# Storing five more output tiles by two DMAs each, in an attention kernel followed by a gated feed-forward

## The chip, the cores and the metric

The kernel runs on one core of a Trainium2 chip. A core has five engines that each work through an instruction queue of their own: TensorE (PE) multiplies matrices into PSUM, VectorE (DVE) and ScalarE (ACT) copy and combine, GpSimd (POOL) copies and issues loads, and SyncE (SP) only issues DMAs and waits. Engines meet through semaphores: an instruction waits until a count is reached, and adds to a count when it is done. The metric is the device time of one execution in microseconds; lower is better. The median of three runs before the change is 219.91 us (219.3 to 221.04).

## The reference, cut to what matters

Batch 8, 8 heads, 512 positions, head width 64, 32 state rows per batch and head; the feed-forward is 512 to 1536 to 512.

```python
a  = softmax(x @ state.T / 8);   xread = a  @ state     # (8, 8, 512, 64)
a2 = softmax(state @ x.T / 8);   sread = a2 @ x         # (8, 8,  32, 64)
t  = concatenate([xread, sread], axis=2)                # 544 rows per batch
t  = t.transpose(0, 2, 1, 3).reshape(8 * 544, 512)
out = (maximum(t @ w_gate, 0) * (t @ w_val)) @ w_out    # (4352, 512) float32
```

## The kernel before, in words

The value product of the attention is folded into the two first weights: for each batch `u_mm` multiplies the state rows by `w_gate` and `w_val` (the tile `U`), and `gv_mm` (line 325) multiplies `U` by the transposed attention weights `ans`. So one group of four matmuls gives the gate and the value of 128 of the 1536 hidden features for the 512 positions of a batch. `relu` (line 354, ACT) and `mult` (line 358, DVE) make the hidden tile `h_sb` from them, and `out_mms` (line 367, PE) multiplies `h_sb` by `w_out`, 128 positions at a time, twelve matmuls to an output tile. The 256 state rows of all batches go through `gvs` (line 347) at the end.

The order of the work is written out by hand. The first batches are a long list of steps (lines 462 to 490). From there a loop (line 561) goes over batch and feature group (`g = 12 * b + jf`); the table at lines 532 to 559 says behind which group the attention of the next batches, the loads and the transposes are put. The output matmuls lag 18 groups behind, in pieces of four (`out_piece`). Three pieces make one tile, and `fin_x` copies it out of PSUM on ACT (line 375) into one of eight `o_sb` buffers and stores it from SP (line 379). There are 32 such tiles, numbered here `4 * b + tsub` from 0 to 31; `fin_x` does 0 to 30. Tiles 23 to 27 are stored by two DMAs of 64 partitions each, the others by one of 128 partitions. Behind the loop come the two tiles of state rows (`fin_s`, lines 381 to 387, which stores from SP and ACT by turns), tile 30, and tile 31 in four column pieces (`out_last`, lines 389 to 400): 256 and 128 columns copied by ACT, 64 and 64 by DVE, stored by SP, ACT, SP, ACT.

SP's queue also holds the DMA transposes: `e_sn<-eT` (line 202), `ans<-a_sn` (line 226), `xT<-xb` (line 154) and `hs_sb<-sn` (line 279). SP's queue around tiles 18 to 22 is: transpose `e_sn` of batch 7, store 18, store 19, transpose `ans` of batch 7, store 20, transpose `hs_sb<-sn` of batches 6 and 7, stores 21, 22, and then the halves of 23.

The DMAs that SP and ACT issue are counted on eight semaphores, dealt out in turn over both queues in the order of the program; each such DMA first waits until the one eight before it has landed. The kernel has 75 of them, so its last one, ACT's store of the last 64 columns of tile 31, counts on the third semaphore (75 = 9 * 8 + 3). At the end of the program (shown under line 605) SP alone waits for all transfers to have landed: a first wait for two of the semaphores of POOL's loads, then eight waits, one for each of the eight semaphores from first to eighth (each paired with another count), then a drain. After that follow a barrier of the five engines, a clearing of the semaphores by POOL, and a second barrier.

Of the kernel before, what the change touches and what calls it, by code (L numbers as in the profile page):

```python
# [16 lines left out]
def kernel(  # L17
# [11 lines left out]
    B, H, S, D = x.shape  # L29
# [340 lines left out]
    def out_rows(b, tsub):  # L370
        return out[b * SP: b * SP + S].rearrange("(p q) m -> q p m", q=NC)[tsub]

    def fin_x(b, tsub, eng="act"):
        o_sb = opool.tile([128, d_model], FP32, name="o_sb", tag="o_sb")
        copy[eng](out=o_sb, in_=held["o", b, tsub])  # L375
        n = 2 if 4 * B - 9 <= 4 * b + tsub < 4 * B - 4 else 1
        for i in range(n):
            rows = slice(128 // n * i, 128 // n * (i + 1))
            nc.sync.dma_start(out=out_rows(b, tsub)[rows], in_=o_sb[rows])
# [26 lines left out]
    def out_piece(b, i):  # L406
        out_part(b, i)
        if i % 3 == 2:
            fin_x(b, i // 3)
# [41 lines left out]
    def x_load_behind(b, gb, gj):  # L451
# [7 lines left out]
             "c": c_unit, "co": c_out, "u": u_unit, "uo": u_out, "gv": gv, "gg": lambda b, jf: g_part(b, jf, 0, (0, 1)), "gw": lambda b, jf: g_part(b, jf, 1, (0, 1)),  # L459
             "ga": lambda b, jf: g_part(b, jf, 0, (0,)), "gb": lambda b, jf: g_part(b, jf, 0, (1,)), "wa": lambda b, jf: g_part(b, jf, 1, (0,)), "wb": lambda b, jf: g_part(b, jf, 1, (1,)), "re": relu, "mu": mult, "o": out_part,  # L460
             "of": fin_x, "xd": x_trans_dma, "ad": att_aT_dma, "xp": x_pad, "sr": lambda b: sr_mm((b,)), "sn": lambda b: sr_norm((b,))}
    program = """
    dx.1.0.2 dx.1.1.2 stc.0.1.dve stc.0.0.dve dw.0.0.128 dw.1.0.128 dw.0.128.128 dw.1.128.128 dw.0.256.256
# [97 lines left out]
    for g in range(first, NF * (B + 1)):  # L561
        b, jf = divmod(g, NF)
# [47 lines left out]
```

## Time and profile before

| what | value |
|---|---|
| median of 3 runs, lowest, highest | 219.91, 219.3, 221.04 us |
| time of the profiled execution | 219.11 us |
| its span, first to last instruction | 217.3 us |
| granted TensorE clock, mean | 0.998 |
| busy DVE | 134.8 us, 62% |
| busy ACT | 117.8 us, 54% |
| busy POOL | 42.5 us, 20% |
| HBM read, written | 18.35 MB, 8.91 MB |

The span is read from one execution, on the slowest (here the only) core. Between the span and the execution's own time lie 1.8 us that the profile's rows do not cover. "SPq" and "ACTq" are the queues of SP and ACT: their rows are issues of DMAs and waits, and are not counted as busy. A row such as "x10: 466/566/589, 173.3 to 194.6" says that there are ten such instructions, with shortest, median and longest duration in ns, and when the first and the last of them began in us. "DMA to landing" is the time from an issue to the last byte's arrival.

### The profile page before, as it was taken

How to read it: one execution, taken by the hardware profiler on the slowest of the kernel's cores; microseconds unless marked ns; L12 is line 12 of the kernel's file. 1: busy time of each engine (PE TensorE's matmuls, PEld its weight loads, DVE VectorE, ACT ScalarE, POOL GpSimd, SP SyncE). 2: the span in 40 equal slices, each digit the busy share in tenths (PEclk: the TensorE clock that was granted, in tenths of full speed). 3: DMA queues.
4: the chain of work that ended last, by engine and by line, in shares of the span. 5: the costliest groups of instructions: out<-in, count | busy, mean ns of one | idle time of the engine just before them, and what ended most of it. 6: DMA issues, size and time to landing. Idle time of an engine off the chain costs nothing.

```text
span 217.3 us, 4841 instructions
## 1 busy us (share of the span) xinstructions
PE 209.4 (96%) x1926; PEld 104.4 (48%) x1952; DVE 134.8 (62%) x233; ACT 117.8 (54%) x225; POOL 42.5 (20%) x63
## 2 busy tenths in 40 slices
PE   8799999999999999999999999999999999999994
PEld 4554454444444444444444444444544445666544
DVE  5799967956887778557966796388745444222100
ACT  4798887737546556455555656454646443333221
POOL 7964059005500431020107000000000000000000
PEclk9999999999999999999999999999999999999999
DMA  7999999488963996919391553131311122222132
GB/s 168 183 195 197 198 230 181 63 148 183 153 170 83 140 163 132 164 52 193 100 148 60 112 132 97 49 99 50 84 28 51 48 48 50 59 58 80 51 97 97
DMA packets 47511, 24.96 MB, mean 115 GB/s; under 512 B 27936, under 2 KB 43168, under 8 KB 47488
## 3 DMA queue, kind: packets, MB, share of 16 engines
q0 software_dynamic: 16896, 9.05, 30.8%
q1 hardware_dynamic: 29696, 14.85, 29.5%
q10 hardware_dynamic: 896, 0.75, 1.4%
q8 instruction: 15, 0.25, 0.5%
q14 instruction: 8, 0.07, 0.1%
HBM read 18.35 MB, written 8.91 MB: 125 GB/s over the span
## 4 chain that ended last, share of the span: by engine, by line
PE 93%; DMA 2%; issue 2%; ACT 1%; DVE 0%; POOL 0%; POOLq 0%
PE o_ps L367 39%; PE gv_ps L325 38%; PE gv_ps L347 5%; PE up L298 4%; DMA xb<-in_x_dram 2%; PE upc L298 2%; PE o_ps L396 1%; PE sr_ps L265 1%; PE sT_ps L189 1%; PE xT_ps L162 1%; PE sc_ps L179 1%; ACT xT L165 0%; PE aT_ps L234 0%; DVE xT L165 0%; ACT e_sn L206 0%
## 5 line engine op out<-in xcount | busy, mean ns | idle before, releaser
L367 PE MATMUL o_ps<-wo_sb,h_sb 128*128 128x512 bf16 x354 | 90.6, 379 | 2.4 <-issue 2.2
L325 PE MATMUL gv_ps<-ans,U 128*128 128x512 bf16 x377 | 92.5, 379 | 0.3
L358 DVE TENSOR_TENSOR h_sb<-gv_ps,g_sb 128x512 bf16<-128x512 f32 x96 | 65.0, 688 | 42.9 <-ACT g_sb L354 41.4
L354 ACT ACTIVATE g_sb<-gv_ps 128x512 bf16<-128x512 f32 (+1 forms) x108 | 61.8, 578 | 51.4 <-PE gv_ps L325 39.2
L325 PEld LDWEIGHTS <-U 128*128 128x128 bf16 x384 | 37.1, 98 | 44.6 <-issue 0.8
L367 PEld LDWEIGHTS <-h_sb 128*128 128x128 bf16 x372 | 35.2, 98 | 42.0 <-issue 4.0
L310 DVE CAST U<-up 128x512 bf16<-128x512 f32 x44 | 27.7, 683 | 5.7 <-PE up L298 5.7
L375 ACT COPY o_sb<-o_ps 128x512 f32<-128x512 f32 x31 | 18.4, 594 | 19.7 <-PE o_ps L367 16.7
L310 ACT CAST U<-up 128x512 bf16<-128x512 f32 x28 | 14.7, 596 | 8.8 <-PE up L298 8.8
L254 POOL COPY xa<-xb 128x1024 bf16<-128x1024 bf16 x16 | 16.0, 1044 | 10.4 <-PE sr_ps L265 5.9
L358 DVE TENSOR_TENSOR hs_sb<-gv_ps,g_sb 128x256 bf16<-128x256 f32 x12 | 5.1, 424 | 15.3 <-PE gv_ps L347 10.4
L212 DVE TENSOR_REDUCE cs<-e_sn 128x16 f32<-128x512 bf16 x16 | 10.8, 675 | 1.2 <-ACT e_sn L206 1.2
L218 DVE TENSOR_TENSOR a_sn<-e_sn,rc 128x512 bf16<-128x512 bf16 x16 | 10.9, 686 | 0.4
L298 PEld LDWEIGHTS <-stT 64*32 64x32 bf16 x560 | 6.8, 91 | 6.4 <-issue 5.3
L320 ACT CAST U<-upc 128x512 bf16<-128x512 f32 (+1 forms) x19 | 8.7, 523 | 1.7 <-PE upc L298 1.7
L453 POOL COPY mark<-g_sb 128x1 bf16<-128x1 bf16 x4 | 0.8, 190 | 41.4 <-ACT g_sb L354 41.4
L197 ACT ACTIVATE eT<-sT_ps 128x512 bf16<-128x512 f32 x10 | 5.4, 594 | 5.2 <-PE sT_ps L189 5.2
L441 POOL DMA_DIRECT2D xb<-in_x_dram x8 | 6.8, 850 | 2.9 <-issue 1.4
L347 PE MATMUL gv_ps<-br,wg_sb 128*128 128x256 bf16 x48 | 7.2, 273 | 0.1
L347 PE MATMUL gv_ps<-br,wv_sb 128*128 128x256 bf16 x48 | 7.2, 273 | 0.0
L399 DVE COPY o_sb<-o_ps 128x64 f32<-128x64 f32 x2 | 0.4, 224 | 10.6 <-PE o_ps L396 10.5
L298 PE MATMUL up<-wg_sb,stT 64*32 64x512 bf16 (+1 forms) x168 | 6.9, 348 | 0.0
(59 smaller groups left out, 122.7 us busy)
## 6 DMA issues: line engine op xcount, KB each, us to landing
out_dram<-o_sb SPq DMA_DIRECT2D x26, 256.0 KB, 2.4
xb<-in_x_dram POOLq DMA_DIRECT2D x6, 512.0 KB, 7.4
wo_sb<-in_moe_w_out_dram POOLq DMA_DIRECT2D x2, 768.0 KB, 10.7
out_dram<-o_sb SPq DMA_DIRECT2D x11, 128.0 KB, 2.3
wg_sb<-in_moe_w_gate_dram POOLq DMA_DIRECT2D x5, 256.0 KB, 9.1
wv_sb<-in_moe_w_val_dram POOLq DMA_DIRECT2D x5, 256.0 KB, 9.7
xb<-in_x_dram POOLq DMA_DIRECT2D x3, 256.0 KB, 5.1
st_f<-in_state_dram POOLq DMA_DIRECT2D x1, 384.0 KB, 11.5
```

The source lines that it names most:

```text
L212: nc.vector.reduce_sum(out=cs, in_=e_v, axis=AX.X)
L218: {"dve": nc.vector, "pool": nc.gpsimd}[eng].tensor_tensor(out=a_sn[b][:, jp].rearrange("p c (j n) -> p c j n", n=Ns), in0=e_v, in1=held[" ...
L254: nc.gpsimd.tensor_copy(out=v[:, hs], in_=xb[b][:, hs])
L298: nc.tensor.matmul(dst[kc][i0:i0 + 32], stT[r:r + 64, parity, b, h], wsb[r:r + 64, j, lo:lo + n], start=True, stop=True)
L310: copy[eng](out=U[b][:, w, kc, lo:lo + 512], in_=held["u", b, w, lo][kc])
L320: copy[eng](out=U[b][:, :, kc, lo:lo + n], in_=held["c", b, lo][kc])
L325: nc.tensor.matmul(ps[w], U[b][:, w, kc, f0:f0 + 128], ANS[b][:, kc].rearrange("p c t -> p (c t)"), start=(kc == 0), stop=(kc == NK - 1))
L347: nc.tensor.matmul(ps[w][:, 0:nt], wsb[:, j, f0:f0 + 128], br[:, j].rearrange("p b n -> p (b n)"), start=(j == 0), stop=(j == NJ - 1))
L354: nc.scalar.activation(out=g_sb[:, 0:n], in_=ps[0][:, 0:n], func=AF.Relu)
L358: nc.vector.tensor_tensor(out=dst, in0=ps[1][:, 0:n], in1=held["g", b, jf][:, 0:n], op=ALU.mult)
L367: nc.tensor.matmul(held["o", b, tsub], src[:, jf, tsub * 128:(tsub + 1) * 128], wo_sb[:, jf], start=(jf == 0), stop=(jf == NF - 1))
L375: copy[eng](out=o_sb, in_=held["o", b, tsub])
```

## The change

The range of tiles that are stored by two DMAs grows from tiles 23 to 27 to tiles 18 to 27. So five more tiles (18 to 22) are stored in two halves of 64 partitions, both issued by SP, one behind the other. The copies, the buffers and the bytes stay what they were.

```diff
     def fin_x(b, tsub, eng="act"):
         o_sb = opool.tile([128, d_model], FP32, name="o_sb", tag="o_sb")
         copy[eng](out=o_sb, in_=held["o", b, tsub])
-        n = 2 if 4 * B - 9 <= 4 * b + tsub < 4 * B - 4 else 1
+        n = 2 if 4 * B - 14 <= 4 * b + tsub < 4 * B - 4 else 1
         for i in range(n):
             rows = slice(128 // n * i, 128 // n * (i + 1))
             nc.sync.dma_start(out=out_rows(b, tsub)[rows], in_=o_sb[rows])
```

The order of instructions on PE, DVE, ACT and POOL does not change; SP has five DMAs more. SP and ACT together issue 80 DMAs (10 * 8), so the last one counts on the eighth semaphore, and every DMA behind tile 18 counts on another semaphore than before. The eight waits at the end keep their order.

## The prediction

> **What bounds the kernel now.** I read the page first: the share of each engine and the chain that ended last.
>
> ```profile
> span 217.3 us, 4841 instructions
> ...
> PE 209.4 (96%) x1926; PEld 104.4 (48%) x1952; DVE 134.8 (62%) x233; ACT 117.8 (54%) x225; POOL 42.5 (20%) x63
> ...
> PE 93%; DMA 2%; issue 2%; ACT 1%; DVE 0%; POOL 0%; POOLq 0%
> ```
>
> PE is busy 96% of the span and is 93% of the chain. Stores are not in it, so a change to stores can matter in two places only: where it makes PE wait, or behind the last matmul. So I read the stretches at the end next, each with its busy time by engine, clock, share of DMA and GB/s.
>
> ```profile
> core 0: us, PE busy (x) PEld busy (x) DVE busy (x) ACT busy (x) POOL busy (x), PEclk, DMA share, GB/s
> 210.00:214.40 4.40, 4.26 (x55) 3.23 (x54) 0.28 (x2) 1.22 (x3) 0.00 (x0) 1.00 0.42 130
> 214.40:216.10 1.70, 0.00 (x0) 0.00 (x0) 0.17 (x1) 0.00 (x0) 0.00 (x0) 1.00 0.46 125
> 216.10:216.42 0.32, 0.00 (x0) 0.00 (x0) 0.00 (x0) 0.00 (x0) 0.00 (x0) 1.00 0.00 0
> 216.42:217.32 0.90, 0.00 (x0) 0.00 (x0) 0.00 (x0) 0.00 (x0) 0.00 (x0) 0.52 0.00 0
> ```
>
> PE stops before 214.40, the last stores move until 216.10, and from there 1.2 us pass in which no engine computes and no byte moves. What fills them stands in the rows of line 605, the end of the program. First 214.50 to 216.10, then 216.11 to 216.42, then 216.15 to 216.45, then 216.48 to the end.
>
> ```profile
> L605 SPq EVENT_SEMAPHORE  x3: 28/28/28, 214.6 to 215.8; - x3
> ```
>
> ```profile
> L605 SPq EVENT_SEMAPHORE  x6: 28/28/28, 216.1 to 216.4; - x6
> ```
>
> ```profile
> L605 SPq EVENT_SEMAPHORE  x5: 28/28/28, 216.2 to 216.4; - x5
> ```
>
> ```profile
> L605 POOLq EVENT_SEMAPHORE  x4: 17/17/17, 216.6 to 217.2; - x4
> L605 SPq DRAIN  x3: 7/7/7, 216.5 to 216.8; - x3
> L605 POOLq EVENT_SEMAPHORE_RANGE_CLEAR  x1: 139/139/139, 216.9 to 216.9; - x1
> ```
>
> These nine waits of SP are the first one on POOL's loads and the eight on the store semaphores. Three of the nine are through by 215.8 (POOL's loads, first, second). The fourth is the third semaphore, on which the last store counts; it begins at 216.1. That this is where the last store lands follows from its issue and its landing:
>
> ```profile
> L400 SPq DMA_DIRECT2D out_dram<-o_sb x2: 332/341/350, 213.4 to 214.2; - x2
> L400 ACTq DMA_DIRECT2D out_dram<-o_sb x2: 357/357/357, 213.9 to 214.6; - x2
> ...
> DMA to landing us min/median/max: 1.5/1.6/1.9
> ```
>
> ACT issues it at 214.6, and with the shortest landing, 1.5 us, it is there at 216.1. Behind it five more waits begin one after the other from 216.2 to 216.4, all for counts that were reached long before, with DMA share 0.00. From the landing to the end everything is serial on SP and then on the barrier.
>
> **The change part by part.** *The last store's semaphore.* It goes from the third to the eighth. The waits for the first seven are then done while the last store is still under way: the stores issued at 213.4, 213.9 and 214.2 land within 1.9 us, by 216.1 at the latest. At the landing only the eighth wait is left, and five waits leave the path. Their price comes from their starts: six waits begin from 216.1 to 216.4, five steps in 0.3 us, 0.06 us each. So 5 * 0.06 = 0.30 us. From below, the duration of a row is 28 ns, which would make 5 * 0.028 = 0.14 us; from above, the whole stretch of 0.32 us without DMA. I take 0.30, since the starts are the serial progress itself and nothing else is in that stretch.
>
> A rule says why the row's duration is too small a price. The Trainium skill, page "Perfetto Trace Analysis", section "Per-engine timelines", says that for an instruction of the sequencer alone the profiler shows only the execution, while fetch, decode and the update of the count lie outside it. By the rows' duration the sum would be 219.77, by the starts 219.61; the starts at 0.06 beside durations of 28 ns agree with the rule.
>
> *Five more issues on SP.* Rows of the stores by one DMA (143 to 170 us) and of those already halved (172 to 196 us):
>
> ```profile
> L379 SPq DMA_DIRECT2D out_dram<-o_sb x5: 332/332/517, 144.8 to 167.6; - x5
> ...
> DMA to landing us min/median/max: 2.1/2.2/2.5
> ```
>
> ```profile
> L379 SPq DMA_DIRECT2D out_dram<-o_sb x10: 466/566/589, 173.3 to 194.6; - x10
> ...
> DMA to landing us min/median/max: 2.2/2.4/3.8
> ```
>
> A pair costs SP 0.466 + 0.589 and a gap of some 0.05 (an estimate: the step between waits above is 0.06 with 28 ns in them), 1.11 us against 0.33: each split tile holds SP 0.78 us longer, five 3.9 us. Behind tiles 21 and 22 only stores are queued. Behind 18 to 20 stand two transposes, and ahead of 18 one more:
>
> ```profile
> L202 SPq DMA_TRANSPOSE e_sn<-eT x1: 1237/1237/1237, 143.5 to 143.5; - x1
> ...
> DMA to landing us min/median/max: 3.1/3.1/3.1
> ```
>
> ```profile
> L212 DVE TENSOR_REDUCE cs<-e_sn x2: 673/674/674, 148.0 to 150.2; 128x16 f32<-128x512 bf16 x2
> ```
>
> ```profile
> L226 SPq EVENT_SEMAPHORE  x1: 1145/1145/1145, 150.8 to 150.8; - x1
> L226 SPq DMA_TRANSPOSE ans<-a_sn x1: 1254/1254/1254, 152.0 to 152.0; - x1
> ...
> DMA to landing us min/median/max: 3.1/3.1/3.1
> ```
>
> ```profile
> L325 PEld LDWEIGHTS <-U x48: 97/98/98, 161.3 to 181.6; 128*128 128x128 bf16 x48
> ```
>
> ```profile
> L279 SPq DMA_TRANSPOSE hs_sb<-sn x1: 1186/1186/1186, 156.7 to 156.7; - x1
> ...
> DMA to landing us min/median/max: 2.3/2.3/2.3
> ```
>
> ```profile
> L283 ACT COPY br<-hs_sb x2: 487/517/547, 166.4 to 166.6; 128x128 bf16<-128x128 bf16 x2
> ```
>
> The `ans` transpose is issued at 152.0, after SP has sat 1145 ns in a wait. So the 0.78 us of tile 19's second half go into that wait first and the transpose does not move. Were it late all the same: it lands at 152.0 + 3.1 = 155.1, and batch 7, whose 48 weight loads begin at 161.3, needs it 6.2 us later. The `hs_sb` transpose is late by 0.78 us, lands at 156.7 + 2.3 + 0.8 = 159.8, and ACT needs it at 166.4: 6.6 us are left. Without this cover each of the two would cost PE up to 0.78 us. The `e_sn` transpose is issued ahead of tile 18, lands at 146.6 and is read at 148.0: 1.4 us of cover, the thinnest here. Cost of all three: nothing.
>
> *Buffers and semaphores.* The second half of a tile is issued about 0.5 us later and lands in at most 3.8 us, so an `o_sb` buffer comes free up to 2.1 us later than now (0.52 + 3.8 against 2.2). ACT's copies show what this meets:
>
> ```profile
> L375 ACT COPY o_sb<-o_ps x10: 585/585/692, 161.7 to 211.7; 128x512 f32<-128x512 f32 x10
> ```
>
> ```profile
> ACT o_sb L375 <- PE o_ps L367: 7.0, 10, 0.9
> ...
> ACT o_sb L384 <- PE o_ps L367: 2.0, 1, 2.0
> ACT o_sb L384 <- DMA out_dram<-o_sb: 2.0, 1, 2.0
> ACT o_sb L375 <- DMA out_dram<-o_sb: 2.0, 1, 2.0
> ```
>
> Ten copies and the two of the state rows lie 4.5 us apart (50 us over 11 gaps); a buffer is used again eight copies later, 36 us. The two waits put down to a DMA are as long as the one for PE beside them, and I read them as waits for PE's twelve matmuls. Each DMA also waits for the one eight before it: with halves that is four tiles, 18 us, against a landing of 3.8. Both cost nothing; without the cover it would be up to 2.1 us per tile on ACT.
>
> *Sum.* On the profiled execution: 219.11 - 0.30 = 218.81 us, its span 217.3 - 0.3 = 217.0. That execution is 0.8 us under the median of the three runs, so for the median I take 219.91 - 0.30 = 219.61, rounded 219.6.
>
> **The rivals.** *Nothing is gained (219.9).* Waits for counts already reached might cost SP nothing once it starts on them earlier, or the barrier might hang on an engine other than SP. For it: 0.3 us is a third of the spread of the three runs. Against it: the five starts from 216.2 to 216.4, and the barrier's first POOL row at 216.6, behind SP's drain at 216.5.
>
> *The change doesn't do what it says.* If the last store counted on the sixth or seventh semaphore, one or two waits of 0.06 us would be left: 219.7. The count of the DMAs speaks against it.
>
> *Slower: the `e_sn` transpose lands late (221.9).* The second half of tile 18 enters the DMA engines while this transpose is still landing (143.5 to 146.6). If its landing grows by over 1.4 us, DVE stands at 148.0 with its multiplies queued behind, and PE follows. The longest landing of a transpose in this profile is 6.1 us, against 2.4:
>
> ```profile
> DMA to landing us min/median/max: 2.3/2.4/6.1
> ```
>
> That would be 3.7 late, 2.3 past the cover: 219.61 + 2.3 = 221.9. Against it: the bytes in flight are the same 256 KB as now, only in two issues.
>
> *Slower: SP's issues come onto the path (223.5).* The 3.9 us of more issue on SP would be lost in full if each issue held up what PE needs next: 219.61 + 3.9 = 223.5. It decides from where a transpose is late by more than its cover, 6.2 us for `ans` and 6.6 for `hs_sb`; the 1.6 us that tiles 18 and 19 add ahead of the one and the 2.3 of tiles 18 to 20 ahead of the other do not reach it even without SP's idle time.
>
> The Trainium skill, page "DMA: Bandwidth & Descriptors", section "Rules for kernel authors", is on the side of this rival: two transfers to disjoint halves of the partitions serialize, so one transfer of 128 is to be used. The issue rows agree that two halves are dearer.
>
> **How the numbers follow.** The forecast has a chance of 0.75, nothing gained 0.14, one or two waits left 0.04, the late transpose 0.05, SP's issues on the path 0.02. The range goes from the profiled execution less the largest gain, 219.11 - 0.32 = 218.8, rounded down to 218.7 for the tenth that the rows' starts are rounded to, to the highest run less the forecast gain, 221.04 - 0.30 = 220.7. It holds the first three cases and leaves the last two out. The forecast alone, without the runs' spread, would reach from 219.59 to 219.77. About 1%, 2.2 us, is what a measurement of this kernel can tell from no change; the first four cases stay within it, the last (1.6%) does not. Beyond these the spread of the runs can cross it, with 0.05 on the fast side and 0.03 on the slow one: faster by over 1% 0.05, within 1% 0.90, slower by over 1% 0.05.
>
> **What would show it.** In the changed profile the waits of line 605 for the first seven semaphores should be through before the last store lands, one wait should begin at the landing, and SP's drain some 0.06 us behind it; from landing to end 0.9 us in place of 1.2. The second halves of tiles 18 to 22 should show ten more rows of 0.47 to 0.59 us, the `ans` transpose should stay at about 152.0 and `hs_sb<-sn` move to 157.4, and PE's busy share and start of line 396 should not move. The forecast is wrong if waits still follow the landing, if PE idles between 145 and 170 us, or if the last store lands later than 1.5 to 1.9 us after its issue.

## The result, and the profile after

The changed kernel takes 219.25 us (median of 22 runs, 218.78 to 220.14), the kernel before 219.75 us (22 runs). The ratio is 0.9975, 95% interval 0.9963 to 0.9987: between 0.29 and 0.81 us less, 0.55 in the middle; the two medians differ by 0.50. The forecast was 0.30 us less and 219.6 us.

The profiled execution of the changed kernel took 219.66 us with a span of 217.9 us, so it is longer than the one profiled before (219.11 and 217.3). A reader who compares only the two spans would find a loss. The stages tell it apart. First the end, in the same four stretches as before (work until PE stops, last stores under way, waits behind the last landing, barrier); the columns are as before. No matmul runs in the last two stretches, so their clock column bears on nothing here.

```profile
core 0: us, PE busy (x) PEld busy (x) DVE busy (x) ACT busy (x) POOL busy (x), PEclk, DMA share, GB/s
210.00:215.28 5.28, 5.18 (x60) 3.63 (x58) 0.29 (x2) 1.76 (x4) 0.00 (x0) 1.00 0.35 110
215.28:216.98 1.70, 0.00 (x0) 0.00 (x0) 0.16 (x1) 0.00 (x0) 0.00 (x0) 1.00 0.45 122
216.98:217.05 0.07, 0.00 (x0) 0.00 (x0) 0.00 (x0) 0.00 (x0) 0.00 (x0) 1.00 0.00 0
217.05:217.88 0.83, 0.00 (x0) 0.00 (x0) 0.00 (x0) 0.00 (x0) 0.00 (x0) 0.74 0.00 0
```

The stretch of waits behind the landing is 0.07 us, and was 0.32. The trace has the landing at 216.97, so from the landing to the end it is 0.91 us here; it was 1.22. SP's waits of line 605, first in 215.40 to 216.90, then in 216.95 to 217.02:

```profile
L605 SPq EVENT_SEMAPHORE  x8: 27/28/28, 215.5 to 216.7; - x8
```

```profile
L605 SPq EVENT_SEMAPHORE  x1: 28/28/28, 217.0 to 217.0; - x1
```

Eight of the nine waits are now through by 216.7, while the last store is still on its way (issued by ACT at 215.5, 1.5 us to land, so there at 217.0). One wait is left at the landing. The last store itself is neither faster nor slower:

```profile
L400 ACTq DMA_DIRECT2D out_dram<-o_sb x2: 357/357/357, 214.8 to 215.5; - x2
...
DMA to landing us min/median/max: 1.5/1.6/1.9
```

The longer span comes from the start. In the chain of work in order of time, before and then after, the transposes of batch 1 on TensorE wait for the load of the first half of batch 1's `x`, which POOL issues (line 441) at 2.66 and 2.68 us; the columns are start, duration in us, and what.

```profile
2.66 5.08 DMA xb<-in_x_dram
```

```profile
2.68 5.94 DMA xb<-in_x_dram
```

This load is the same instruction in both kernels, over 130 us ahead of anything that the change touches, and it took 0.86 us longer in this execution. From the first weight load of line 325 to the last one of line 396, nothing has moved. Before, then after:

```profile
L325 PEld LDWEIGHTS <-U x384: 94/98/99, 12.8 to 181.6; 128*128 128x128 bf16 x192
```

```profile
L396 PEld LDWEIGHTS <-h_sb x48: 97/98/98, 211.3 to 214.1; 128*128 128x128 bf16 x48
```

```profile
L325 PEld LDWEIGHTS <-U x384: 95/98/99, 13.7 to 182.4; 128*128 128x128 bf16 x192
```

```profile
L396 PEld LDWEIGHTS <-h_sb x48: 98/98/98, 212.1 to 215.0; 128*128 128x128 bf16 x48
```

From 12.8 to 214.1 and from 13.7 to 215.0 it is 201.3 us both times. From there to the last landing it is 2.01 us both times. So the two spans differ by about 0.9 us more at the start and 0.31 us less at the end.

The pages give PE 209.4 us (96%) before and this after:

```profile
PE 212.9 (98%) x1952; PEld 104.7 (48%) x1952; DVE 134.9 (62%) x233; ACT 117.9 (54%) x225; POOL 42.6 (20%) x63
```

That is no change of the kernel: the trace before has 1926 matmuls, this one 1952, beside 1952 weight loads in both, so 26 matmuls are missing from the record before.

### The profile page after: what moved, and what is told of

It is laid out like the page before. It is cut to its first block, busy times and chain, and to the rows that moved or that the text cites. A ratio compares the mean times of both kernels' runs of the same rounds, so it can differ in the third digit from the quotient of the medians.

```text
span 217.9 us, 4872 instructions
## 1 busy us (share of the span) xinstructions
PE 212.9 (98%) x1952; PEld 104.7 (48%) x1952; DVE 134.9 (62%) x233; ACT 117.9 (54%) x225; POOL 42.6 (20%) x63
## 4 chain that ended last, share of the span: by engine, by line
PE 94%; DMA 3%; issue 1%; ACT 1%; DVE 0%; POOL 0%; POOLq 0%
PE o_ps L367 40%; PE gv_ps L325 38%; PE gv_ps L347 5%; PE up L298 4%; DMA xb<-in_x_dram 3%; PE upc L298 2%; PE o_ps L396 1%; PE sr_ps L265 1%; PE sT_ps L189 1%; PE xT_ps L162 1%; PE sc_ps L179 1%; ACT xT L165 0%; PE aT_ps L234 0%; DVE xT L165 0%; ACT e_sn L206 0%
## 5 line engine op out<-in xcount | busy, mean ns | idle before, releaser
L367 PE MATMUL o_ps<-wo_sb,h_sb 128*128 128x512 bf16 x372 | 94.3, 379 | 0.0
```

The lines of the kernel that those rows point to most:

```text
L367: nc.tensor.matmul(held["o", b, tsub], src[:, jf, tsub * 128:(tsub + 1) * 128], wo_sb[:, jf], start=(jf == 0), stop=(jf == NF - 1))
```

## The experiments

Two theories stood. By the theory of the place, all of the gain is the number of waits behind the last landing, 0.06 us each. By the rival, the splitting of stores does something to the time by itself: a gain (the 0.55 us measured are more than the 0.30 forecast), or a loss where SP's longer issue reaches the path. Six further kernels vary the place and the splits apart from each other, and the change itself ran again. Each has twelve runs, beside 35 (the first four below) or 29 runs of the kernel before. The ratios are the measured ones with their intervals; they need not equal the quotient of the two medians. In the two with extra loads the lines behind the edit are three higher, so line 605 is 608 there.

**The place alone.** No tile more is split; five small loads that nobody reads are put behind stores 18 to 22.

```diff
             nc.sync.dma_start(out=out_rows(b, tsub)[rows], in_=o_sb[rows])
+        k = 4 * b + tsub - 18
+        if 0 <= k < 5:
+            nc.sync.dma_start(out=touch[16 * k:16 * k + 16, 0], in_=x[k, 0, 0:16, 0:8])
```

> No tile more is split than before; SP issues five small loads (16 partitions of 32 bytes, into a tile that nobody reads) behind the stores of tiles 18 to 22, so that the last store counts on the eighth semaphore. Theory of the place (each wait behind the last landing costs 0.06 us): 0.30 us less than before (ratio 0.9986), and 0.91 us from the last landing to the end of the span, as in the changed kernel. Rival, the split itself gains something (stores in halves): no gain of its own here, so the ratio is 1.000, or if both act, about half of the 0.55 us that the change measured.

Measured: ratio 0.9979 (0.9964 to 0.9993), 0.46 us less. One of the twelve runs took 565.08 us, for a reason that no trace here shows; the ratio is of the other eleven. The medians, 219.7 and 219.76 us, lie closer together than the ratio says, so the rows carry more weight here than the time. One wait stands behind the landing (window 216.99 to 217.05), and 0.93 us pass from there to the end:

```profile
L608 SPq EVENT_SEMAPHORE  x1: 28/28/28, 217.0 to 217.0; - x1
```

```profile
216.98:217.91 0.93, 0.00 (x0) 0.00 (x0) 0.00 (x0) 0.00 (x0) 0.00 (x0) 0.62 0.00 0
```

A gain without any further split: the rival's 1.000 lies outside the interval, and the stretch behind the landing is as short as in the change.

**The splits alone.** Tiles 18 to 22 are split as in the change, and three such loads bring the last store back to the third semaphore (83 DMAs).

```diff
-        n = 2 if 4 * B - 9 <= 4 * b + tsub < 4 * B - 4 else 1
+        n = 2 if 4 * B - 14 <= 4 * b + tsub < 4 * B - 4 else 1
...
+        if 0 <= k < 3:
```

> Tiles 18 to 22 are split as in the change, and three small loads are put behind the stores of 18 to 20, so that the last store stays on the third semaphore. Theory of the place: same as before (ratio 1.000), 1.22 us from the last landing to the end. Rival, the split itself gains: 0.25 to 0.55 us less than before (ratio 0.9975 to 0.9989) with 1.22 us behind the landing. Rival, the split costs SP time that comes onto the path: slower by up to 3.9 us.

Measured: ratio 1.0001 (0.9985 to 1.0016). Six waits from the landing on (window 216.70 to 217.07), as before the change, and 1.22 us to the end:

```profile
L608 SPq EVENT_SEMAPHORE  x6: 28/28/28, 216.7 to 217.0; - x6
```

```profile
216.69:217.91 1.22, 0.00 (x0) 0.00 (x0) 0.00 (x0) 0.00 (x0) 0.00 (x0) 1.00 0.00 0
```

The splits, with the three small loads beside them, gain nothing and cost nothing that this measurement can tell (from 0.33 us less to 0.35 us more).

**Fewer splits, same place.** Only tiles 26 and 27 are split, 72 DMAs.

```diff
-        n = 2 if 4 * B - 9 <= 4 * b + tsub < 4 * B - 4 else 1
+        n = 2 if 4 * B - 6 <= 4 * b + tsub < 4 * B - 4 else 1
```

> The other way round: tiles 23 to 25 are stored whole, so only 26 and 27 are split; 72 DMAs, the last on the eighth semaphore. Theory of the place: 0.30 us less than before (ratio 0.9986), 0.91 us from the landing to the end. Rival, splits gain: slower than before by 0.15 to 0.33 us from three splits less, or that much less gain.

Measured: ratio 0.9985 (0.9973 to 0.9998), 0.33 us less, and 0.92 us behind the landing:

```profile
216.86:217.78 0.92, 0.00 (x0) 0.00 (x0) 0.00 (x0) 0.00 (x0) 0.00 (x0) 1.00 0.00 0
```

So the same place is reached with three DMAs less instead of five more, and it gains. A loss from the missing splits is not seen.

**The change again, on the same chip as these three.**

> The changed kernel again, beside the others on one chip. Theory of the place: 0.30 us less than before (ratio 0.9986). If the 0.55 us measured at first hold, the ratio is 0.9975, and 0.25 us come from something else than the waits.

Measured: ratio 0.9981 (0.9967 to 0.9995), 0.42 us less (the medians, 219.62 and 219.76, are 0.14 apart), 0.92 us behind the landing (216.51 to 217.43). Between the 0.30 and the 0.55; its interval holds both, so this run does not tell them apart.

**The first semaphore.** Tiles 17 to 27 are split (`4 * B - 15` in the same line), 81 DMAs.

> Six more tiles split than before (17 to 27), 81 DMAs: the last store counts on the first semaphore. Theory of the place: seven waits stand behind the last landing, 7 * 0.06 + 0.91 = 1.33 us from the landing to the end, 0.12 us slower than before (ratio 1.0006). Rival, splits gain: faster than before, by 0.3 to 0.66 us (ratio 0.997 to 0.9986).

Measured: ratio 1.0015 (1.0004 to 1.0026), 0.33 us more, between 0.09 and 0.57. From the landing on there are eight waits (window 216.75 to 217.25), one for the landing and seven behind it, and 1.35 us to the end:

```profile
L605 SPq EVENT_SEMAPHORE  x8: 28/28/28, 216.8 to 217.2; - x8
```

```profile
216.74:218.09 1.35, 0.00 (x0) 0.00 (x0) 0.00 (x0) 0.00 (x0) 0.00 (x0) 0.89 0.00 0
```

One split more than the change turns its gain into a loss. This is what the rival cannot give.

**The fifth semaphore.** Tiles 21 to 27 are split (`4 * B - 11`), 77 DMAs.

> Two more tiles split than before (21 to 27), 77 DMAs: the last store counts on the fifth semaphore. Theory of the place: three waits behind the landing, 3 * 0.06 + 0.91 = 1.09 us to the end, 0.12 us less than before (ratio 0.9994). Rival, splits gain: 0.1 to 0.22 us less, with 1.22 us behind the landing.

Measured: ratio 0.9999 (0.9987 to 1.0012). The time does not decide: the expected 0.9994 and no change both lie in the interval. The rows do: four waits from the landing on (window 216.45 to 216.70) and 1.11 us to the end.

```profile
L605 SPq EVENT_SEMAPHORE  x4: 28/28/28, 216.5 to 216.6; - x4
```

```profile
216.44:217.55 1.11, 0.00 (x0) 0.00 (x0) 0.00 (x0) 0.00 (x0) 0.00 (x0) 1.00 0.00 0
```

**Many more splits, same place as the change.** Tiles 10 to 27 are split (`4 * B - 22`), 88 DMAs.

> Thirteen more tiles split than before (10 to 27), 88 DMAs: the last store counts on the eighth semaphore. Theory of the place: 0.30 us less than before, as in the change (ratio 0.9986), 0.91 us behind the landing; SP's 13 * 0.78 = 10 us more of issue are hidden. Rival, SP's issue comes onto the path: slower than the change, by up to 8 us; if only the transposes of batches 5 and 6 are held up past their cover, by 1 to 2 us.

Measured: ratio 0.9985 (0.9972 to 0.9998), 0.33 us less, 0.93 us behind the landing. SP has 26 issues in place of 13 for tiles 10 to 22, and the first weight load of line 325 and the last one of line 396 are still 201.3 us apart:

```profile
L325 PEld LDWEIGHTS <-U x384: 95/98/99, 13.2 to 182.0; 128*128 128x128 bf16 x192
```

```profile
L396 PEld LDWEIGHTS <-h_sb x48: 97/98/98, 211.7 to 214.5; 128*128 128x128 bf16 x48
```

So the cover of SP's issue holds for eighteen split tiles, not only for ten.

Together:

| last store on semaphore | split tiles | waits behind the landing | landing to end, us | ratio (95%) |
|---|---|---|---|---|
| first | 17 to 27 | 7 | 1.35 | 1.0015 (1.0004 to 1.0026) |
| third, before | 23 to 27 | 5 | 1.22 | 1 |
| third, splits alone | 18 to 27 | 5 | 1.22 | 1.0001 (0.9985 to 1.0016) |
| fifth | 21 to 27 | 3 | 1.11 | 0.9999 (0.9987 to 1.0012) |
| eighth, the change | 18 to 27 | 0 | 0.91 | 0.9975 (0.9963 to 0.9987) |
| eighth, the change again | 18 to 27 | 0 | 0.92 | 0.9981 (0.9967 to 0.9995) |
| eighth, place alone | 23 to 27 | 0 | 0.93 | 0.9979 (0.9964 to 0.9993) |
| eighth, fewer splits | 26, 27 | 0 | 0.92 | 0.9985 (0.9973 to 0.9998) |
| eighth, many splits | 10 to 27 | 0 | 0.93 | 0.9985 (0.9972 to 0.9998) |

From seven waits to none, 1.35 - 0.92 = 0.43 us, that is 0.06 us for each wait. Every interval holds the time that this price gives (1.0006, 1, 0.9994 and 0.9986 for the first, third, fifth and eighth).

## Why the prediction was right

*The price of a wait.* The starts gave 0.06 us, the row's duration 0.028. The landing-to-end times of four places give 0.06. Pricing the wait by its own row would have halved the gain; the row shows only a part of what the wait holds SP for. This agrees with the Trainium skill, page "Perfetto Trace Analysis", section "Per-engine timelines", by which the row of such an instruction shows only its execution.

*The sum.* 0.30 us were forecast, and 1.22 - 0.91 = 0.31 us are missing between landing and end. The runs gave 0.55 us at first, with 0.30 just inside the interval, and 0.42, 0.46, 0.33 and 0.33 in the four later measurements of the same place. The five are not independent, since some share the runs of the kernel before, and they lie a little above 0.30. By the means of the same runs it is 0.51 us less at first and 0.31, 0.33, 0.38 and 0.30 later. Whether something comes on top of the waits stays open. In all nine traces the first weight load of line 325 and the last of line 396 are 201.3 us apart and the last store lands 2.0 us after that, so it could lie only ahead of the former, where the start varies from 12.8 to 13.7 us and hides it.

*The level.* 219.61 us were forecast and 219.25 measured. Of these 0.36 us, 0.16 come from the kernel before, whose median of three runs (219.91) stood above that of 22 (219.75), and 0.20 from the gain. The range of 218.7 to 220.7 would have held without any gain too; what tests the forecast is the ratio and the stretch behind the landing.

*SP's issues.* Each pair was to hold SP 0.78 us longer. The `ans` transpose was to stay where it was, with the delay eaten by a wait in front of it, and `hs_sb<-sn` to move by 0.78 us. These are the rows after; first the ten halves of tiles 18 to 22:

```profile
L379 SPq DMA_DIRECT2D out_dram<-o_sb x10: 466/514/593, 145.7 to 169.0; - x10
...
DMA to landing us min/median/max: 2.2/2.3/2.6
```

```profile
L226 SPq EVENT_SEMAPHORE  x1: 374/374/374, 152.4 to 152.4; - x1
L226 SPq DMA_TRANSPOSE ans<-a_sn x1: 1282/1282/1282, 152.9 to 152.9; - x1
```

```profile
L279 SPq DMA_TRANSPOSE hs_sb<-sn x1: 1223/1223/1223, 158.3 to 158.3; - x1
```

The wait went from 1145 to 374 ns, 0.77 us less, and the transpose went from 152.0 to 152.9, which is the 0.9 us of the start and nothing more. `hs_sb<-sn` went from 156.7 to 158.3, 1.6 us, of which 0.7 to 0.8 are the splits. The forecast's step holds for both, and many more splits did not reach the path either. The buffers hold nothing up longer either: ACT's two waits that were put down to a DMA are 2.0 us each, as before.

*The rivals.* "Nothing is gained" is outside the interval of every kernel with the last store on the eighth semaphore. "One or two waits are left" is refuted by the one row at 217.0. The `e_sn` transpose did not land late: it is issued at 144.4 and lands 3.0 us later, as before (3.1). SP's issues on the path cost nothing here: a split tile is dearer to issue (0.47 to 0.59 us for each half against 0.33 for the whole), but the kernel does not wait for it. The Trainium skill, page "DMA: Bandwidth & Descriptors", section "Rules for kernel authors", advises against two transfers to disjoint halves of the partitions. The split by itself gained nothing here (1.0001), as that rule has it, and cost nothing that was measured.

The row of the `e_sn` transpose after the change:

```profile
L202 SPq DMA_TRANSPOSE e_sn<-eT x1: 1232/1232/1232, 144.4 to 144.4; - x1
...
DMA to landing us min/median/max: 3.0/3.0/3.0
```

One expectation was off in a way that matters to a reader: a single profile's span was to fall to 217.0, and it was 217.9. The span of one execution is no measure of a change of 0.3 us where the start alone varies by 0.9.

## What to carry to other kernels

Look at what follows the last landing. Where one queue waits for several counts in a fixed order, the transfer that ends last should be counted on the one that is waited for last; every wait behind it costs 0.06 us here even though its count was reached long ago. The place is set by the number of transfers, modulo the number of counts, so any edit that adds or drops a transfer moves it: one split more than this change made the kernel slower, and three splits fewer than before gained as much as five more, as far as these runs can tell, with fewer instructions.

## What the runs showed of the hardware

Between two executions of nearly the same program the load of the first half of batch 1's `x` took 5.08 and 5.94 us to land, with the same DMAs issued ahead of it. The first weight load of line 325 came 0.9 us later with it, and no later stage made that up: from there to the last weight load of line 396 it is 201.3 us in the kernel before, in the changed one and in all seven other traces, and TensorE is busy for 96 to 98% of each span.

A wait of SP for a count that had long been reached shows 28 ns in its row and kept SP from the next one for 0.06 us. From the start of the last such wait to the end of the span 0.90 to 0.92 us pass in all nine traces, whichever semaphore the last store counts on.
